# Outputs of twelve chunks as one stacked f16 product per head in a fused mLSTM and mixture-of-experts kernel

## The chip, the cores and the metric

The kernel runs on one core of one Trainium2 chip. The metric is the device time of one execution in microseconds (us), as the median of three runs. The engines are named as the profile names them: PE is the matrix engine (PEld its weight loads), DVE the vector engine, ACT the scalar engine, POOL is GpSimd, SP the engine that issues most DMAs (SPq its queue).

## The reference, cut to what matters

There are 4 sequences (b) of 768 tokens with 8 heads of width 40. Each head keeps a state, every token reads it, and the results become rows of 320 numbers. Each row then goes to the one of eight experts that a router picks.

```python
for t in range(S):
    m_new = np.maximum(f_gate[:, :, t] + m, i_gate[:, :, t])
    f_stab = np.exp(f_gate[:, :, t] + m - m_new)
    i_stab = np.exp(i_gate[:, :, t] - m_new)
    m = m_new
    C = f_stab[..., None, None] * C + i_stab[..., None, None] * einsum('bhd,bhe->bhde', vt, kt)
    n = f_stab[..., None] * n + i_stab[..., None] * kt
    h_tilde = einsum('bhde,bhe->bhd', C, qt)
    denom = np.maximum(np.abs(einsum('bhd,bhd->bh', n, qt)), 1.0)[..., None]
    y[:, :, t] = sigmoid(o_gate[:, :, t]) * h_tilde / denom
x = y.transpose(0, 2, 1, 3).reshape(3072, 320)
logits = x @ w_gate + modality_bias[modality_id]
e_idx, gate_w = argmax(logits), softmax(logits)[e_idx]
out[mask_e] = gate_w[mask_e] * (relu(x[mask_e] @ w1[e]) @ w2[e])
```

## The kernel before

With these gates the state of a head no longer changes after the first 64 tokens of its sequence. `still_arm` builds that state S (the 40 columns of C and the vector n, 41 columns per head) from 64 tokens, and reads it for all later ones. A second arm, which does the general recurrence, stands behind a branch on a word that a check leaves; it is not run here.

**Chunks.** The 3072 tokens are 24 chunks of 128. Chunks 0 to 21 are light: their output is a product of the chunk's queries with S. Chunks 0 to 5 belong to b=0, 5 to 10 to b=1, 11 to 16 to b=2, 16 to 21 to b=3 (5 and 16 are half and half). Chunks 22 and 23 hold the first 64 tokens of every sequence (`special`).

**Light products.** S lies block-diagonal, three heads to a group: 120 rows by 123 columns. `light` (L1984) does one f32 product for each of three groups. From chunk 14 on (`SPLIT = 7` pairs of chunks) `light16` (L2006) does three f16 products a group in its place: high part of q by high part of S, high by low, low by high. The high parts are made by ACT, the low parts by DVE (L2003 and L2004 for a pair of chunks' queries, L1896 and L1897 for a state).

**Behind a chunk.** DVE multiplies the output by its gate (L2039) and the denominators (L2032 to L2037), POOL scales it (L2055), ACT rounds it to f16 (L2057), DVE forms the remainder (L2059), and POOL's indirect DMA scatters the rows to x_s in DRAM (L2066), ordered by modality, so that rows for one expert lie together.

**Experts.** Almost all rows of one modality go to one expert, so two experts (A and B) have their weights loaded (L1968) and split in a high and a low f16 part by ACT (L1969) and DVE (L1970). Rows are worked in 14 tiles in the order of `STREAM`: A0, then A1 and A2 together, then eleven tiles of 256 rows, B0, B1, A3, B2, A4 and so on. The first three tiles take their columns from SBUF by selection products (L2193); the others by a DMA transpose of x_s on SP's queue (L2161). A tile has a first layer (L2295 for whole blocks of 128 inputs, L2303 for the last 64), whose results ACT turns into hh (L2283) and DVE into the remainder hl (L2284), and a second layer (L2340): 16 products with hh, then 8 with hl, for each 128 rows. The router's products are L2233.

**Order.** Every step is a task of a `Plan`. The sequence of tasks on each engine is read from a string of numbers (`ORDER`), and each engine works its own list strictly in that order; PE takes a light product where the list has it, between an expert's products, and waits there if its queries or states aren't ready. Where the plan sees a gap on PE, products with zeros are put in (L2537).

Of the kernel before, what the change touches and what calls it, by code (L numbers as in the profile page):

```python
# [1563 lines left out]
SPLIT = 7  # L1564
# [33 lines left out]
    "-f-g-h-k-l-o-p-s-t-w-x-y-z-{-|.#.$.%.&.'.(.-.../.2.3.6.7.:.;.>.?.@.A.B.C.F.G,s.H.I.J.K.Q.R.S.V.W.Z.[._.`.c.d.e.f.g.h.k.l"
    ".m.n.o.p.u.v.w.z.{.~/#/&/'/*/+/,/--8/.///2/3/4/5/6/7-=#)#{#+#U%r#?#}#,#2#/#*#3#4#<#5#7#8#@#I#B#|#J#K#A#L#D#C#W#E#N#M#F#V"
    "#G#O#Q#Y$N%-$L$c#P%/$J$,$($)$*$-$+$>$.$B$?$C$@$0$A$4$~$%${$z%#$1$|$5$F$}$G%w%z%v%{$Q#f&,#c&-%x#i$e%&%y&.&f%'&/&0&1&M#l&h"  # L1600
    "&k#o#r#u#x&O$T&V&X%2&~&z&y&}&{&|$U$V$W$h$i&4$j$k$^$Y&5%5%6%7%~&#$_$`'E'=$Z'A'I%G'd&s%8%J%D%>'%%M'Q(,&j%:$q&r%?'g'&%P'c%@"
# [69 lines left out]
def still_arm(tc, a, out):  # L1671
# [123 lines left out]
    def load_q(i):  # L1795
        dma(393, lambda: sy.dma_start(qg[i % 4], a["ql"][:, 2 * i:2 * i + 2]), w=[f"qg{i % 4}"])
# [208 lines left out]

    def light16(c, n, y):  # L2006
        if c % 2 == 0:
            split_q(c // 2)
# [677 lines left out]
```

## Time and profile before

| what | value |
|---|---|
| median of 3 runs | 211.71 us (210.97 to 212.02) |
| profiled execution | 210.83 us, span 208.9 us |
| PE busy | 198.2 us (95% of the span) |
| DVE busy | 129.1 us (62%) |
| ACT busy | 98.0 us (47%) |
| POOL busy | 76.1 us (36%) |
| bytes moved by DMA | 30.72 MB |
| granted PE clock, mean | 0.992 |

The span runs from the first to the last instruction; the profiled execution's time is 1.9 us more than that. Busy shares are averages over the whole span. Until about 58 us of the trace the states, the light chunks, the weights of two experts and the first tiles overlap; after it the tiles set the rhythm.

### The profile page before, as it was taken

Reading aid. Unit: us, or ns where it says so; the run is one execution under the profiler, and the core shown is the slowest. Engines: PE = TensorE matmul, PEld = TensorE weight load, DVE = VectorE, ACT = ScalarE, POOL = GpSimd, SP = SyncE. Lnnn points to the kernel's source line nnn. Section 1 sums busy time; section 2 is a strip of 40 time slices with the busy share of each in tenths; the row PEclk is TensorE's granted clock in tenths of the full one; section 3 lists DMA queues with packets and bytes.
Section 4 is the critical chain, followed back from the end, with each engine's and each line's share of the span. In section 5 each row is a group of like instructions: output and inputs, shape, how many; then the busy total and the mean of one; then the engine's idle time right before and its main releaser. Section 6 shows DMA issues by size and latency. Waiting matters only on the chain. (4 is left out here: it accounts for less than half of the span.)

```text
span 208.9 us, 5296 instructions
## 1 busy us (share of the span) xinstructions
PE 198.2 (95%) x2063; PEld 155.8 (75%) x2064; DVE 129.1 (62%) x446; ACT 98.0 (47%) x202; POOL 76.1 (36%) x84
## 2 busy tenths in 40 slices
PE   6879999999999999999999999999999999999960
PEld 2569979878788788778778787787787877878640
DVE  7999797998967737665576406028961521595600
ACT  3579688867687419455425205343141321411320
POOL 5035772652448363634183253000302305020231
PEclk9999999999999999999999999999999999999996
DMA  5999995968784851266211328500101105930000
GB/s 180 349 397 403 399 385 160 288 261 223 161 264 142 132 132 55 79 125 163 46 63 72 89 81 217 93 3 0 64 2 63 34 31 178 313 142 3 31 33 27
DMA packets 27111, 30.72 MB, mean 147 GB/s; under 512 B 19190, under 2 KB 19480, under 8 KB 26824
## 3 DMA queue, kind: packets, MB, share of 16 engines
q1 hardware_dynamic: 24520, 22.06, 36.4%
q0 software_dynamic: 2416, 8.13, 11.1%
q8 instruction: 17, 0.28, 0.5%
q10 hardware_dynamic: 144, 0.13, 0.2%
q14 instruction: 14, 0.11, 0.2%
HBM read 18.57 MB, written 8.22 MB: 128 GB/s over the span
## 5 line engine op out<-in xcount | busy, mean ns | idle before, releaser
L2355 POOL DMA_INDIRECT out<-ob,ois x25 | 24.7, 990 | 77.8 <-ACT ob L2353 27.1
L2340 PEld LDWEIGHTS <-hh 128*128 128x128 f16 (+1 forms) x400 | 37.7, 99 | 14.0 <-issue 0.3
L2284 DVE SCALAR_TENSOR_TENSOR hl<-H,hh 128x512 f16<-128x512 f32 (+2 forms) x40 | 25.5, 649 | 35.8 <-ACT hh L2283 34.4
L2283 ACT ACTIVATE hh<-H 128x512 f16<-128x512 f32 (+2 forms) x40 | 22.1, 567 | 46.0 <-PE H L2295 28.4
L2066 POOL DMA_INDIRECT x_s<-rows,pos_i x24 | 25.7, 1072 | 28.3 <-ACT Sh L1896 4.0
L2353 ACT ACTIVATE ob<-O,zs 128x320 f32<-128x320 f32 x24 | 12.6, 525 | 34.2 <-PE O L2340 9.5
L2340 PE MATMUL O<-w2hA,hh 128*128 128x320 f16 (+1 forms) x104 | 27.8, 299 | 0.0
L2340 PE MATMUL O<-w2lA,hh 128*128 128x320 f16 (+1 forms) x104 | 27.8, 299 | 0.0
L2340 PE MATMUL O<-w2hB,hh 128*128 128x320 f16 x96 | 26.5, 299 | 0.0
L2340 PE MATMUL O<-w2lB,hh 128*128 128x320 f16 x96 | 26.5, 299 | 0.0
L2295 PE MATMUL H<-xt,w1hA 128*128 128x256 f16 (+2 forms) x176 | 26.4, 259 | 0.0
L2340 PEld LDWEIGHTS <-hl 128*128 128x128 f16 (+1 forms) x200 | 18.8, 98 | 7.8 <-issue 0.7
L2295 PE MATMUL H<-xt,w1hB 128*128 128x256 f16 x144 | 24.4, 273 | 0.0
L2295 PEld LDWEIGHTS <-w1hA 128*128 128x128 f16 x224 | 20.3, 98 | 2.9 <-issue 0.6
L2295 PE MATMUL H<-xt,w1lA 128*128 128x256 f16 (+2 forms) x88 | 22.1, 259 | 0.0
L2295 PEld LDWEIGHTS <-w1hB 128*128 128x128 f16 x192 | 18.0, 98 | 3.5 <-issue 1.3
L2295 PE MATMUL H<-xt,w1lB 128*128 128x256 f16 x72 | 19.6, 273 | 0.0
L2055 POOL TENSOR_TENSOR xr<-xr,ab 128x640 f32<-128x640 f32 x11 | 14.8, 1344 | 10.0 <-DVE ab L2037 9.9
L2340 PE MATMUL O<-w2hA,hl 128*128 128x320 f16 (+1 forms) x104 | 16.1, 299 | 0.0
L2340 PE MATMUL O<-w2hB,hl 128*128 128x320 f16 x96 | 15.2, 299 | 0.0
L1996 PE MATMUL Y<-S,qg 120*128 120x123 f32 (+3 forms) x90 | 11.2, 277 | 1.6 <-DVE ab L2032 0.8
L2059 DVE TENSOR_TENSOR rows<-xr,rows 128x128 f16<-128x128 f32 (+1 forms) x22 | 10.1, 478 | 3.9 <-ACT rows L2057 3.9
(215 smaller groups left out, 381.0 us busy)
## 6 DMA issues: line engine op xcount, KB each, us to landing
qg<-in_ql SPq DMA_DIRECT2D x11, 384.0 KB
og<-in_ogl SPq DMA_DIRECT2D x12, 320.0 KB
stage<-in_w1s SPq DMA_DIRECT2D x8, 320.0 KB
stage<-in_w SPq DMA_DIRECT2D x8, 320.0 KB
stage<-in_w1t SPq DMA_DIRECT2D x1, 1280.0 KB
og<-in_w SPq DMA_DIRECT2D x1, 1280.0 KB
kvs<-in_kvs SPq DMA_DIRECT2D x2, 364.5 KB
sp<-in_spq SPq DMA_DIRECT2D x4, 160.0 KB
```

What stands on the lines that cost most here:

```text
L1996: t_.matmul(y[p0:p1, HQ * g:HQ * g + w], lhsT=q[0:k, i, g, p0:p1], rhs=Ss[b][0:k, g, 0:w], start=(g == 0), stop=(g == 2), skip_group_check ...
L2055: on(640, lambda: by.tensor_tensor(x3, x3, ab.rearrange("p c h o -> p (c h) o").broadcast_to([P, 2 * H, D]), ALU.mult), r=abk, w=xk)
L2059: two(2 * (z - a0), lambda a0=a0, z=z, o=o: v.tensor_tensor(rows[:, cs, o:o + z - a0], xr[:, :, a0:z], rows[:, cs, a0:z], ALU.subtract), r ...
L2066: ins = g_.indirect_dma_start(out=x_s[:, :], out_offset=bass.IndirectOffsetOnAxis(ap=pos_i[:, c:c + 1].bitcast(U32), axis=0), in_=rows[:, ...
L2283: act(g * n, lambda: s_.activation(hh[:, sl, 0:n], hp3, AF.Relu), r=[nb], w=[f"hh{j}{i}" for i in fs])
L2284: dve(g * n, lambda: v.scalar_tensor_tensor(hl[:, sl, 0:n], hp3, 0.0, hh[:, sl, 0:n], ALU.max, ALU.subtract), r=[nb] + [f"hh{j}{i}" for i ...
L2295: t_.matmul(dst, lhsT=w[:, i, ws], rhs=x[:, xb], start=(first and b == 0 and q == 0), stop=(last and b == 1 and q == 2), skip_group_check= ...
L2340: t_.matmul(op[p0:p0 + nr, 0:DM], lhsT=t[:, at[f], o_:o_ + nr], rhs=w[:, f], start=(i < ways), stop=(i >= 24 - ways), skip_group_check=True)
L2353: act(DM + 80, lambda op=op, o=o, qc=qc, nr=nr: s_.mul(obs[o][0:nr], op[0:nr, 0:DM], facs[0:nr, qc:qc + 1]), r=[no, f"fac{m_}"], w=[f"ob{o}"])
L2355: swdma(164, lambda o=o, qc=qc, nr=nr: disjoint("outf", g_.indirect_dma_start(out=out[:, :], out_offset=bass.IndirectOffsetOnAxis(ap=ois[0 ...
```

## The change

`SPLIT` goes from 7 to 5, so the f16 form begins at chunk 10. In that form a chunk's queries are loaded threefold (`q3`: 120 rows, three copies of a head's 40 query elements, 8 heads by 128 tokens, 512 KB a chunk, one DMA for each chunk, where a pair of chunks was 384 KB). ACT writes the high part to all 120 rows, and DVE overwrites rows 0 to 39 with the low part. The state is laid out as 120 rows by 41 columns a head: high, high, low. One product over 120 rows gives low q by high S, high q by high S and high q by low S at once: 8 products of 41 columns for a chunk, in place of 9 of 123 and 82.

The stacked state comes from a new function, `stack_states`: ACT and DVE split the unmasked 120 by 369 block (for b=2 and b=3 straight from PSUM, for which the masking by DVE, L1892, falls away), one DMA writes both parts to DRAM, and three DMAs read the diagonal blocks back (40 rows each, runs of 574 bytes). `split_q`, which did a pair of chunks, is gone. Some tiles share memory (tri with a stacked state, gb with the f32 states, aw with kws, Wt with gt), the router's weights get the flag for the shared port in the plan (L2468), and all five engines get new sequences.

```diff
-SPLIT = 7
+SPLIT = 5
...
     def load_q(i):
-        dma(393, lambda: sy.dma_start(qg[i % 4], a["ql"][:, 2 * i:2 * i + 2]), w=[f"qg{i % 4}"])
+        if i < SPLIT:
+            dma(393, lambda: sy.dma_start(qg[i % 4], a["ql"][:, 2 * i:2 * i + 2]), w=[f"qg{i % 4}"])
+            return
+        for c in (2 * i, 2 * i + 1):
+            n, j = c - 2 * SPLIT, (c - 2 * SPLIT) % 3
+            dma(524, lambda j=j, n=n: sy.dma_start(qf[j], a["q3"][:, n]), w=[f"qf{j}"] + ([f"qg{j}", f"qg{j + 1}"] if n < 3 else []))
...
+    def stack_states(b, src, key):
+        d = S_d[b - 1]
+        act(3 * HQ, lambda: s_.mul(S16[:, 0], src, SSC), r=[key], w=["Sh"])
+        (two if b == 1 else dve)(3 * HQ, lambda: v.scalar_tensor_tensor(S16[:, 1], src, SSC, S16[:, 0], ALU.mult, ALU.subtract),
+                                 r=[key, "Sh"], w=["Sl"])
+        dma(180, lambda: sy.dma_start(d[0:120 * 6 * HQ].rearrange("(p x) -> p x", p=120), S16.rearrange("p h g n -> p (h g n)")),
+            r=["Sh", "Sl"], w=[f"S_d{b}"] + (["tri"] if b == 1 else []))
+        n = D * 6 * HQ
+        blocks = d[0:3 * (n + DV)].rearrange("(j x) -> j x", j=3)[:, 0:n].rearrange("j (d h n) -> h d j n", d=D, h=2)
+        for e, x in enumerate((0, 0, 1)):
+            dma(82, lambda e=e, x=x: sy.dma_start(Sst[b][D * e:D * e + D], blocks[x][:, :, 0:2 * HQ + DV]), r=[f"S_d{b}"], w=[f"T{b}{e}"])
...
     def light16(c, n, y):
-        if c % 2 == 0:
-            split_q(c // 2)
-        (qh, ql), i, j = q16[c // 2 % 2], c % 2, c // 2 % 2
+        j = (c - 2 * SPLIT) % 3
+        act(H * P, lambda: s_.mul(qst[j][0:120], qf[j][0:120], QSC), r=[f"qf{j}"], w=[f"qh{j}"])
+        two(H * P, lambda: v.scalar_tensor_tensor(qst[j][0:D], qf[j][0:D], QSC, qst[j][0:D], ALU.mult, ALU.subtract), r=[f"qf{j}"], w=[f"qh{j}"])
 
         def mm():
-            for g in range(3):
+            for h in range(H):
+                g, u = divmod(h, 3)
                 for p0, p1, b in spans(c):
-                    k, w = (120, HQ) if g < 2 else (80, 2 * DV)
-                    Sh, Sl = S16[b]
-                    for t, (a, z) in enumerate(((qh, Sh), (qh, Sl), (ql, Sh))):
-                        t_.matmul(y[p0:p1, HQ * g:HQ * g + w], lhsT=a[0:k, i, g, p0:p1], rhs=z[0:k, g, 0:w],
-                                  start=(g == 0 and t == 0), stop=(g == 2 and t == 2), skip_group_check=True)
+                    t_.matmul(y[p0:p1, DV * h:DV * h + DV], lhsT=qst[j][0:120, h, p0:p1], rhs=Sst[b][0:120, u, HQ * g:HQ * g + DV],
+                              start=(h == 0), stop=(h == H - 1), skip_group_check=True)
...
 ORDER = (
-    "#=#>#:#X$&$'$<$=$x$y%t$K%u$M$O&*&+$a$b$d$S&G&H&I&J&K&P%+%,%.%0&g&Q&R&S&T&w&Y&x&Z&[&]&^$g&_'9':';%4'>'?'B'C'F'G'a'b'J'K'L"
+    "#=#>#:#X$$$%$:$;$v$w%r%s$I$K$M&/&.$_$`$b&K&L&M$Q&N&O%)%*%,%.&T&U&V&W&X&l$e&^&_&`&a&b&c'H'I'J'M'N'Q'R'U'V'Y'Z'[']%2'('^'_"
```

What the new sequences move is seen at three places.

On PE, between the first and the second layer of A1 with A2 (Y are the banks of the light products, O and H those of the experts). Before, chunks 12 and 13 stand there in f32:

```order
L2295 MATMUL O_66<-xt_105,w1lA 128x192
L1996 MATMUL Y_69<-S_120,qg_79 128x123 x2
L1996 MATMUL Y_69<-S_120,qg_79 128x82
L1996 MATMUL Y_70<-S_120,qg_79 128x123 x2
L1996 MATMUL Y_70<-S_120,qg_79 128x82
L2340 LDWEIGHTS hh_112
```

Now chunk 10 stands a little later, behind the 16 products with hh and the router's five and ahead of the first with hl; the pair of rows for a head comes eight times:

```order
L2353 MATMUL O_67<-w2lA,hh_109 64x320
...
L2246 LDWEIGHTS xt_102
L2246 MATMUL M_68<-wgr,xt_102 128x16
L2030 LDWEIGHTS qst_78
L2030 MATMUL Y_69<-Sst_85,qst_78 128x41
...
L2353 LDWEIGHTS hl_111
```

Chunks 10 and 11 stood before and inside the second layer of A0, and 12 and 13 here; now 10 is here, 11 behind B0's first layer, and 12 and 13 in B1's first layer. All four have left the stretch ahead of B0 but chunk 10.

On DVE, the stretch ahead of the remainders of A1 with A2. Before (w1lB are the low parts of B's first-layer weights):

```order
L2059 TENSOR_TENSOR rows<-xr_158,rows 128x2x256
L2253 TENSOR_SCALAR gsm_178<-gsm_178 128x1
L2254 RECIPROCAL zs<-gsm_178 128x1
L2284 SCALAR_TENSOR_TENSOR hl_114<-H_65,hh_112 128x2x192
L2284 SCALAR_TENSOR_TENSOR hl_114<-H_63,hh_112 128x2x192
L2248 TENSOR_REDUCE zs<-ky_174 128x1
L2284 SCALAR_TENSOR_TENSOR hl_114<-H_64,hh_112 128x2x192
L2284 SCALAR_TENSOR_TENSOR hl_114<-O_66,hh_112 128x2x192
L1970 SCALAR_TENSOR_TENSOR w1lB<-stage,w1hB 128x640
```

After (S_81 is a state's low part, qst a chunk's queries):

```order
L1911 SCALAR_TENSOR_TENSOR S_81<-Y_69,S_81 120x369
L2072 TENSOR_TENSOR rows<-xr_151,rows 128x2x256
L2257 TENSOR_TENSOR lg_161<-lg_161,mxx_167 128x8
L2024 SCALAR_TENSOR_TENSOR qst_78<-qg,qst_78 40x1024
L2254 SCALAR_TENSOR_TENSOR lg_162<-lg_162,bias 64x8
L2265 TENSOR_REDUCE gsm_169<-ex_163 128x1
L1990 SCALAR_TENSOR_TENSOR w1lB<-stage,w1hB 128x640
L2266 TENSOR_SCALAR gsm_169<-gsm_169 128x1
L2050 RECIPROCAL ab_149<-ab_149 128x16
L2267 RECIPROCAL zs<-gsm_169 128x1
L1990 SCALAR_TENSOR_TENSOR w1lB<-stage,w1hB 128x640
L2297 SCALAR_TENSOR_TENSOR hl_111<-H_63,hh_109 128x2x192
```

A state's low part, one chunk's queries and two of B's weights have moved ahead of the remainders.

On SP, from B's first weights to B0's transpose and on. Before:

```order
L1968 DMA stage<-in_w1s 128x640
L1796 DMA qg_80<-in_ql 128x768
L1968 ISA
L1968 DMA stage<-in_w 128x640
L1799 DMA og<-in_ogl 128x640
L2161 DMA_TRANSPOSE xt_107<-x_s 128x5x256
L1968 ISA
L1968 DMA stage<-in_w 128x640
```

After (S_d are the states in DRAM, Sst the stacked ones in SBUF):

```order
L1918 DMA Sst_85<-S_d_82 40x3x287
L1988 ISA
L1988 DMA stage<-in_w1s 128x640
L2174 DMA_TRANSPOSE xt_104<-x_s 128x5x256
L1913 DMA S_d_83<-S_81 120x738
L1806 DMA qg<-in_q 128x1024
L1988 ISA
L1988 DMA stage<-in_w 128x640
...
L2175 DMA zs<-x_s 128x2x1
L1918 DMA Sst_86<-S_d_83 40x3x287
```

The reads of the state of b=1 now stand ahead of B0's transpose, and those of b=2 behind the last of B's weights, ahead of B1's transpose.

## Rows read from the trace of the kernel before

**Rows 1.** The page's first lines: span, busy time of the engines.

```profile
span 208.9 us, 5296 instructions
PE 198.2 (95%) x2063; PEld 155.8 (75%) x2064; DVE 129.1 (62%) x446; ACT 98.0 (47%) x202; POOL 76.1 (36%) x84
```

**Rows 2.** Windows: stretch, its length, busy time per engine, clock, DMA share.

```profile
16.00:43.40 27.40, 27.40 (x364) 23.52 (x361) 24.73 (x78) 23.56 (x50) 16.75 (x15) 1.00 0.93 329
58.00:88.00 30.00, 30.00 (x327) 23.93 (x325) 19.22 (x65) 17.68 (x35) 16.89 (x16) 1.00 0.51 135
118.00:203.60 85.60, 84.02 (x783) 65.17 (x781) 39.23 (x134) 25.73 (x54) 18.09 (x19) 1.00 0.26 79
```

**Rows 3.** Timeline of PE, 26 to 39 us (start, us, line, operation): f32 chunks 10 to 13.

```profile
26.72 0.90 PE L1996 MATMUL Y<-S,qg 120*128 120x123 f32 x6
27.45 0.30 PE L2340 MATMUL O<-w2hA,hh 128*128 128x320 f16 x1
...
28.00 0.80 PE L1996 MATMUL Y<-S,qg 120*128 120x123 f32 x6
28.63 0.30 PE L2340 MATMUL O<-w2hA,hh 128*128 128x320 f16 x1
...
37.00 1.49 PE L1996 MATMUL Y<-S,qg 120*128 120x123 f32 x12
38.42 0.32 PE L2340 MATMUL O<-w2hA,hh 128*64 128x320 f16 x1
```

**Rows 4.** Timeline of PE, 65 to 73 us: f16 chunk 16, then another.

```profile
65.73 0.25 PE L2017 MATMUL Y<-Sh,qh 120*64 120x123 f16 x2
...
66.30 0.31 PE L2340 MATMUL O<-w2hB,hh 128*128 128x320 f16 x1
...
72.00 0.22 PE L2017 MATMUL Y<-Sh,qh 120*128 120x123 f16 x1
...
72.33 0.20 PE L2017 MATMUL Y<-Sh,qh 80*128 80x82 f16 x1
...
72.44 1.25 PE L2340 MATMUL O<-w2hB,hl 128*128 128x320 f16 x8
```

**Rows 5.** Timeline of PE at 77 us: the router's ten products, and what follows.

```profile
77.23 0.41 PE L2233 MATMUL M<-wgr,xt 128*128 128x16 f16 x10
77.49 0.38 PE L2295 MATMUL H<-xt,w1hA 128*128 128x256 f16 x2
```

**Rows 6.** Groups by form, PEld: weight loads of f16 light products (busy, mean ns).

```profile
L2017 PEld LDWEIGHTS <-qh 120*128 120x128 f16 x28 | 2.3, 98 | 0.2
```

**Rows 7.** Groups by form, DVE and ACT: splits of queries, states and weights.

```profile
L2004 DVE SCALAR_TENSOR_TENSOR ql<-qg,qh 120x768 f16<-120x768 f32 x4 | 3.8, 953 | 0.8 <-ACT qh L2003 0.8
L1970 DVE SCALAR_TENSOR_TENSOR w1lB<-stage,w1hB 128x640 f16<-128x640 f32 x4 | 3.2, 818 | 0.0
L1897 DVE SCALAR_TENSOR_TENSOR Sl<-S,Sh 120x369 f16<-120x369 f32 x3 | 1.6, 539 | 0.0
L1892 DVE TENSOR_TENSOR S<-Y,mask 120x369 f32<-120x369 f32 x2 | 1.0, 538 | 0.0
L2003 ACT ACTIVATE qh<-qg 120x768 f16<-120x768 f32 x4 | 3.3, 837 | 0.0
```

**Rows 8.** Timeline of DVE, 13 to 39 us: router's weights, A's and the remainders.

```profile
13.92 0.87 DVE L2468 SCALAR_TENSOR_TENSOR wgr<-cst,wgr 128x24 f16<-128x24 f32 x1
...
26.30 3.06 DVE L1970 SCALAR_TENSOR_TENSOR w2lA<-stage,w2hA 128x640 f16<-128x640 f32 x4
...
36.73 1.02 DVE L2284 SCALAR_TENSOR_TENSOR hl<-H,hh 128x384 f16<-128x384 f32 x2 [0.88 <-ACT hh L2283]
...
38.20 0.55 DVE L2284 SCALAR_TENSOR_TENSOR hl<-O,hh 128x384 f16<-128x384 f32 x1
```

**Rows 9.** Timeline of SP's queue, 38 to 46 us: a write to DRAM and its reader.

```profile
38.80 0.43 SPq L2481 DMA_DIRECT2D g_d<-G  x1
45.14 0.51 SPq L2096 DMA_DIRECT2D gb<-g_d  x1
```

More of the change, by code (lines that the diff above doesn't have):

```diff
@@ L1598 @@
[L1598 to L1601, printed above, removed]
@@ L1742, in still_arm @@
     kvs = [tl([P, 9 * D + 9 * DV], F32, f"kvs{i}") for i in range(2)]
-    qg = [tl([P, 2, 3, P], F32, f"qg{i}") for i in range(4)]
-    q16 = [[tl([120, 2, 3, P], F16, f"q{n}{i}") for n in "hl"] for i in range(2)]
-    S16 = [None] * B if SPLIT > 10 else [None] + [[tl([120, 3, HQ], F16, f"S{n}{b}") for n in "hl"] for b in range(1, B)]
+    qgs = tl([P, 4 * 6 * P], F32, "qg")
+    qg = [qgs[:, 6 * P * i:6 * P * (i + 1)].rearrange("p (c g t) -> p c g t", c=2, g=3) for i in range(4)]
+    qf = [qgs[:, H * P * i:H * P * (i + 1)].rearrange("p (h t) -> p h t", h=H) for i in range(3)]
+    qst = [tl([P, H, P], F16, f"qst{i}") for i in range(3)]
+    S16 = tl([120, 2, 3, HQ], F16, "S16")
+    S_d = [dr.tile([3 * (D * 6 * HQ + DV)], F16, name=f"S_d{b}") for b in range(1, B)]
+    Sst = [None] + [tl([P, 3, 2 * HQ + DV], F16, f"Sst{b}") for b in range(1, B)]
     ogs = tl([P, NOG * 2 * DM], F32, "og")
@@ L1767, in still_arm @@
     obs = [tl([P, DM], F32, f"ob{i}") for i in range(3)]
-    Ss = [tl([P, 3, HQ], F32, f"S{b}") for b in range(3)]
-    Ss.append(Ss[0])
+    Ss2 = tl([P, 2, 3, HQ], F32, "S")
+    Ss = [Ss2[:, b] for b in range(2)]
     ident = tl([32, 32], F32, "ident")
-    tri = tl([P, P], BF16, "tri")
+    tri = Sst[1].rearrange("p j n -> p (j n)")[:, 0:P].bitcast(BF16)
     ones = tl([P, P], BF16, "ones")
@@ L1808, in still_arm @@
     kw = [kws[:, i] for i in range(2)]
-    m, gt, G, Bs, Wt = (tl([32, FT], F32, n) for n in ("m", "gt", "G", "Bs", "Wt"))
+    m, gt, G, Bs = (tl([32, FT], F32, n) for n in ("m", "gt", "G", "Bs"))
+    Wt = gt
     zz = tl([P, P], BF16, "zz")
@@ L2083, in prefill @@
         dma(84, lambda: sy.dma_start(x_s[NX - SPARE:NX], zrow[0:SPARE]), r=["zrow", "zid"], w=["prefill"])
-    gb = small([H, FT], "gb")
-    aw = small([H, FT], "aw")
+    gb, aw = (t.rearrange(f, **k)[:, 0:H * FT].rearrange("p (h t) -> p h t", h=H)
+              for t, f, k in ((Ss2, "p b g n -> p (b g n)", {}), (kws, "p b h d -> p (b h d)", {})))
     bT = small([16], "bT")
@@ L2467, in still_arm @@
     act(24, lambda: s_.mul(wgr[:, :, 0], wg_sb, WSC), r=["cst"], w=["wgh"])
[L2468 removed]
+    two(24, lambda: v.scalar_tensor_tensor(wgr[:, :, 1], wg_sb, WSC, wgr[:, :, 0], ALU.mult, ALU.subtract), r=["cst", "wgh"], w=["wgr"])
     done = [0]
@@ L2628, in _layout_still @@
     qt = q.transpose(0, 2, 1, 3)[b_, t_]
-    ql = np.zeros((P, 22, 3, P), np.float32)
+    ql = np.zeros((P, 2 * SPLIT, 3, P), np.float32)
+    q3 = np.zeros((P, 22 - 2 * SPLIT, H, P), np.float32)
+    for e in range(3):
+        q3[D * e:D * e + D] = qt[2 * SPLIT:22].transpose(3, 0, 2, 1)
     for h in range(H):
         g, j = divmod(h, 3)
-        ql[D * j:D * (j + 1), :, g] = qt[0:22, :, h].transpose(2, 0, 1)
+        ql[D * j:D * (j + 1), :, g] = qt[0:2 * SPLIT, :, h].transpose(2, 0, 1)
     ogl = o.transpose(0, 2, 1, 3)[b_, t_].reshape(NC, P, DM).transpose(1, 0, 2)
```

65 lines of the change are left out of this document (32 added, 33 removed).

## The prediction

> **What bounds the kernel now.** I began with the page's busy times: PE is at work in 198.2 of 208.9 us, no other engine in more than 62% [rows 1]. Such a share is an average, so next came the windows, cut at 16 us (PE's last wait) and at 43.4 us (start of B0). The reader is to see there that PE's busy time equals the length of the stretch from 16 to 43.4 us and from 58 to 88 us, and that its clock stands at 1.00 of full speed, the 2.4 GHz level, in all of them [rows 2]. In the stretch to 203.6 us it lacks 1.58 us [rows 2], at its end: PE stops at about 202.0, and only the last output is left. So what PE no longer has to do after 16 us is worth its full time, as long as no other engine then comes too late. That is a real condition from 16 to 43.4 us: there DVE is busy for 24.73 and ACT for 23.56 of 27.4 us, and the DMA engines for 0.93 of the time. From 58 to 88 us DVE has 19.22 of 30 and ACT 17.68, with the DMA engines at 0.51 [rows 2]; after 118 us both are mostly idle.
>
> **What PE loses.** I take a step's time on PE as the distance from its first product to the next step's first, since products overlap. The f32 chunks 10 to 13 take 27.45 - 26.72 = 0.73, 28.63 - 28.00 = 0.63 and, two together, 38.42 - 37.00 = 1.42 us: 2.78 us [rows 3]. An f16 chunk takes 72.44 - 72.00 = 0.44 us, and chunk 16, whose two halves run side by side, 66.30 - 65.73 = 0.57 [rows 4]. Chunks 14, 15 and 17 to 21 make seven of the first kind: 3.08 + 0.57 = 3.65 us. In all 6.43 us fall away.
>
> **What PE gets.** Eleven chunks of 8 products with 41 columns, and 16 half-wide ones for chunk 16. The trace has no product of f16 with 41 columns, but has it between two rows with the same full weight load: the router's ten products of 16 columns take 77.49 - 77.23 = 0.26 us, 0.026 each [rows 5], and the three of 82 columns 72.44 - 72.33 = 0.11, 0.037 each [rows 4]. 41 columns are nearer to 16; I take 0.030. Then 88 products are 2.64 us, and chunk 16 is 8 pairs at 0.030 plus the 0.13 by which it exceeds a whole chunk today, 0.37: together 3.0 us (2.6 by the lower row, 3.7 by the upper). Net, PE has 6.43 - 3.0 = 3.4 us less to do (2.7 to 3.8). 2.5 of it (2.78 less chunk 10's new 0.24) lie ahead of B0, 0.9 behind its start.
>
> A page speaks against this price. The Trainium skill, "TensorE: Matmul & The Clock Gate", section "Back-to-back issue gap", gives about 81 ns for each product of 128 columns in a sustained stream of load and product; the six of 123 columns here take (72.33 - 72.00) / 6 = 55 ns [rows 4], so the measurement decides. At 81 ns the new products would be 7.9 us and PE would have 1.5 us more to do, about 213.9 us.
>
> **What is lost on the way.** The early 2.5 us count only if DVE delivers earlier too, and two places are close. First, A0's second layer uses A's second-layer remainders, four pieces of 0.77 us from 26.30 to 29.36 [rows 8], a piece each 0.55 us (28.00 - 27.45 [rows 3]). Today two f32 chunks stretch that use; without them PE comes to the fourth piece nearly a us before 29.36. DVE reaches the pieces earlier as well: two maskings are gone (1.0 us [rows 7]) and the router's remainder (0.87, for 24 columns [rows 8]) is moved away, against one state's remainder of 0.54 [rows 7]. I put the loss there at 0.3. Second, the remainders of A1 with A2 end at 38.75 today, with 0.88 us of DVE's waiting ahead of them [rows 8]. In the new list a state's remainder (0.54), one chunk's queries (0.953 for 768 columns, so about 1.27 for 1024) and two of B's pieces (2 x 0.82) stand ahead of them [rows 7], while two chunks' gating and denominators have gone. PE wants them 1 to 2 us earlier. I put 0.4 there. So 0.7 us lost: bounds 0 (DVE always in time) and 2.5 (B0 starts at 43.4 as before).
>
> **What I cost at nothing.** The queries' splits: 12 chunks at 1.27 on DVE and 1.12 on ACT (0.837 for 768 [rows 7]) are 15.2 and 13.4 us, in place of 3.8 and 3.3 [rows 7]: some 11 and 10 us more. All but the first chunk's stand between B0's start and the end of B2, where about 40% of either engine is free by the stretch from 58 to 88 us [rows 2]; in a tile of (202.0 - 43.4) / 11 = 14.4 us there are three or four such chunks, 4 to 5 us. Remainders (hl) may wait behind one for 1.3 us; 16 products with hh come ahead of them on PE, four times 0.55, 2.2 us [rows 3]. If that cover went, each us of a late chunk would be a us of PE. Transfers: 12 x 512 KB for 6 x 384 KB, with the states some 5 MB more, some 14 us of the DMA engines at the 354 GB/s that 329 at a share of 0.93 come to; half their time is free at 58 to 88 us [rows 2]. The router's remainder is a gain of up to 0.7 us on DVE, which I have counted within the loss above.
>
> **Sum.** 3.4 - 0.7 = 2.7 us less. The profiled execution's 210.83 us (1.9 us around a span of 208.9) would become 208.1, the span 206.2; that execution lies 0.9 below the median of 211.71, from which I forecast 209.0.
>
> **Rivals.**
> 1. *The saving mostly arrives* (the forecast), 207.5 to 210.3. For it: PE's full stretches [rows 2] and that later tiles have idle engines. Against: the two close places. Chance 0.65.
> 2. *DVE and ACT set B0's start.* Their 90% and 86% before 43.4 us [rows 2] stay, PE waits where the f32 chunks stood and only the late 0.9 us counts: 210.8 (210.3 to 211.9). Against it: their lists ahead of B0 have two chunks less behind the products. Chance 0.16.
> 3. *The states come late through SP's queue*, the one on the other side. The state of b=2 is written to DRAM behind B0's transpose, at about 36 us, and three reads wait for that write on SP, with the state of b=3 and B1's transpose queued behind them. PE stops at chunk 11, at the end of B0's first layer, near 48 us. A write and the read behind it are seen once: issued at 38.80, the reader let go at 45.14, 6.3 us [rows 9]. That makes 42.3 for the reads, and 48.6 if they need as long to land: just about in time. It decides for slower when the states land 3.8 us after PE wants them (the 2.7 us gained plus 1.1), past 52 us, that is with some 8 us each way; then about 213.2. Against it: the 6.3 us include a queue full of weights. Chance 0.08.
> 4. *The products don't become cheaper by their columns.* At the 123-column spacing of 0.055 they are 5.4 us, the net gain 1.0 and with the loss 0.3: 211.4, chance 0.05. If the weight loads (98 ns [rows 6]) stood bare, 9.5 us, 215.5 us, chance 0.03: the router's 26 ns speak against it.
> The remaining 0.03 is for a larger gain, below 207.5, if DVE's head start shortens the first 16 us too.
>
> **How the numbers follow.** The point is rival 1's, 209.0. The range from 207.3 to 211.9 holds cases 1, 2 and the milder half of 4, and most of the last 0.03: 0.86 by these chances; I leave it there because the loss's bounds (0 to 2.5) and the products' (2.7 to 3.8) put 207.9 and 211.5 inside. 0.5%, about 1.1 us, is what a measurement can tell from no change. Faster by more than that (under 210.65): case 1, a third of case 2 at most, and the last 0.03: 0.70. Within: the rest of case 2 and the 211.4: 0.18. Slower: 3, the bare loads, and a little for what no row shows: 0.12.
>
> **What would show it.** Products of L2030 about 0.03 us apart, 0.24 us a chunk. B0's first product at 41 to 42 us in place of 43.4, with PE's first gaps after 16 us in A0's and A1/A2's second layers, released by DVE hl or w2lA. From B0 to the end 0.2 us less than today's 158.6 (0.9 gained, 0.7 for chunks 11 to 13). No wait of PE at L2030. Wrong would make it: a wait for qst or Sst there, B0 still at 43.4, or L2030 at 0.055 us and more.

## The result, and the profile after

| | before | after |
|---|---|---|
| median, us | 211.70 (4 runs, 210.97 to 212.02) | 208.21 (4 runs, 207.99 to 209.25) |
| profiled execution, its span | 210.83, 208.9 | 207.99, 206.1 |
| DMA, MB | 30.72 | 35.81 |

The ratio is 0.985, 95% interval 0.9808 to 0.9891: faster by 1.1 to 1.9%, where 209.0 us (0.987) was forecast. The changed kernel, run again later, gave 0.989 (e5). Lines of the kernel have moved by 11 to 20; the products of `light` are L2016, those of `light16` L2030, the experts' second layer L2353.

The page of the changed kernel, first lines, for [rows 1]: PE has 3.0 us less, DVE 12.4 and ACT 9.1 more.

```profile
span 206.1 us, 5360 instructions
PE 195.2 (95%) x2064; PEld 152.6 (74%) x2064; DVE 141.5 (69%) x452; ACT 107.1 (52%) x210; POOL 84.8 (41%) x84
```

Its windows, cut at B0's new start (stretch, length, PE, PEld, DVE, ACT, POOL busy, clock, DMA share, GB/s), for [rows 2]:

```profile
16.00:41.67 25.67, 24.56 (x338) 20.18 (x336) 24.86 (x65) 20.66 (x41) 18.08 (x15) 1.00 0.96 313
41.67:58.00 16.33, 16.33 (x182) 13.17 (x181) 15.06 (x50) 13.40 (x25) 9.20 (x7) 1.00 0.93 282
58.00:88.00 30.00, 29.95 (x345) 23.40 (x342) 21.82 (x70) 20.26 (x36) 15.71 (x14) 1.00 0.86 245
118.00:200.80 82.80, 81.14 (x783) 63.23 (x777) 44.36 (x146) 29.33 (x62) 19.92 (x21) 1.00 0.31 85
```

PE is full from B0 on. Ahead of B0 it now lacks 1.11 us, where it lacked nothing. The DMA share from 58 to 88 us is 0.86, not 0.51.

PE's timeline shows both sums (for [rows 3, 4]; a bracket is the idle time ahead and what ended it):

```profile
16.08 0.54 PE L2552 MATMUL M<-zz 128*128 128x512 bf16 x2
16.46 0.44 PE L2206 MATMUL O<-sel,rows 128*128 128x128 f16 x5
...
18.04 1.57 PE L2016 MATMUL Y<-S,qg 120*128 120x123 f32 x12 [0.85 <-DVE xr L2052]
...
27.72 0.30 PE L2353 MATMUL O<-w2lA,hh 128*128 128x320 f16 x1 [0.25 <-DVE w2lA L1990]
...
37.45 0.36 PE L2030 MATMUL Y<-Sst,qst 120*128 120x41 f16 x8
37.74 0.73 PE L2353 MATMUL O<-w2hA,hl 128*64 128x320 f16 x8
...
41.67 0.38 PE L2308 MATMUL H<-xt,w1hB 128*128 128x256 f16 x2
...
65.54 0.36 PE L2030 MATMUL Y<-Sst,qst 120*128 120x41 f16 x8
65.75 1.25 PE L2353 MATMUL O<-w2hB,hl 128*128 128x320 f16 x8
...
73.44 0.74 PE L2030 MATMUL Y<-Sst,qst 120*64 120x41 f16 x24
74.02 0.38 PE L2308 MATMUL H<-xt,w1hA 128*128 128x256 f16 x2
...
198.98 0.17 PE L2467 MATMUL M<-bsum,ones 128*128 128x1 bf16 x1
```

A stacked chunk takes 0.29 or 0.30 us at three places (37.45 to 37.74 is one), 0.20 to 0.22 at seven (65.54 to 65.75 is one), and chunks 16 and 17 together take 0.58. B0 starts at 41.67, 1.77 earlier than before. PE's one new long wait, 0.85 us ahead of chunk 8, is for DVE. DVE's timeline and POOL's there (for [rows 8]):

```profile
16.44 1.15 DVE L1957 TENSOR_SCALAR ss<-cumx 128x2 f32<-128x2 f32 x1
17.51 0.87 DVE L2052 SCALAR_TENSOR_TENSOR xr<-og,Y 128x320 f32<-128x320 f32 x2
...
24.91 2.03 DVE L1990 SCALAR_TENSOR_TENSOR w2lA<-stage,w2hA 128x640 f16<-128x640 f32 x1
```

```profile
15.99 1.58 POOL L2068 TENSOR_TENSOR xr<-xr,ab 128x640 f32<-128x640 f32 x1 [1.41 <-DVE ab L2050]
...
24.97 1.27 POOL L2068 TENSOR_TENSOR xr<-xr,ab 128x640 f32<-128x640 f32 x1
```

A comparison of two columns lasts 1.15 us and ends at 17.59, as POOL's scaling does (17.57); a piece of A's remainders lasts 2.03 where its neighbours take 0.81, and POOL scales then too. PE's waits of 0.85 and 0.25 us stand behind these two. In the kernel before, the same comparison stood well ahead of POOL's scaling, and the new list has moved it:

```profile
7.28 0.16 DVE L1937 TENSOR_SCALAR ss<-cumx 128x2 f32<-128x2 f32 x1
```

### The profile page after: what moved, and what is told of

The parts are those of the page before. It is cut to its first block, busy times and chain, and to the rows that moved or that the text cites. A ratio compares the mean times of both kernels' runs of the same rounds, so it can differ in the third digit from the quotient of the medians.

```text
span 206.1 us, 5360 instructions
## 1 busy us (share of the span) xinstructions
PE 195.2 (95%) x2064; PEld 152.6 (74%) x2064; DVE 141.5 (69%) x452; ACT 107.1 (52%) x210; POOL 84.8 (41%) x84
## 2 busy tenths in 40 slices
DMA packets 29551, 35.81 MB, mean 174 GB/s; under 512 B 19421, under 2 KB 21151, under 8 KB 29263
## 4 chain that ended last, share of the span: by engine, by line
PE 77%; DVE 8%; DMA 6%; issue 2%; ACT 2%; SPq 1%; POOL 0%; POOLq 0%; DVEq 0%; ACTq 0%
PE O L2353 36%; PE H L2308 21%; PE H L2316 7%; PE O L2308 7%; DMA out<-ob,ois 3%; DMA og<-in_ogl 3%; DVE xr L2052 2%; PE M L2246 1%; PE Y L2016 1%; PE Y L2030 1%; PE Y L2135 1%; ACT og L1996 1%; PE Y L2120 1%; DVE w1lA L1990 1%; DVE rows L2072 1%
## 5 line engine op out<-in xcount | busy, mean ns | idle before, releaser
L2368 POOL DMA_INDIRECT out<-ob,ois x25 | 28.3, 1134 | 62.3 <-DVE zs L2261 21.4
L2353 PEld LDWEIGHTS <-hh 128*128 128x128 f16 (+1 forms) x400 | 37.7, 98 | 15.0 <-issue 1.0
L2079 POOL DMA_INDIRECT x_s<-rows,pos_i x24 | 30.2, 1259 | 23.3 <-ACT ob L2366 4.0
L2353 PE MATMUL O<-w2lA,hh 128*128 128x320 f16 (+1 forms) x104 | 27.8, 299 | 0.3 <-DVE w2lA L1990 0.3
L2353 PE MATMUL O<-w2hA,hh 128*128 128x320 f16 (+1 forms) x104 | 27.8, 300 | 0.0
L2353 PE MATMUL O<-w2hB,hh 128*128 128x320 f16 x96 | 26.5, 299 | 0.1
L2353 PE MATMUL O<-w2lB,hh 128*128 128x320 f16 x96 | 26.5, 299 | 0.0
L2353 PEld LDWEIGHTS <-hl 128*128 128x128 f16 (+1 forms) x200 | 18.7, 98 | 7.7 <-issue 0.7
L2353 PE MATMUL O<-w2hA,hl 128*128 128x320 f16 (+1 forms) x104 | 15.8, 300 | 0.0
L2353 PE MATMUL O<-w2hB,hl 128*128 128x320 f16 x96 | 15.3, 299 | 0.0
L2024 DVE SCALAR_TENSOR_TENSOR qst<-qg,qst 40x1024 f16<-40x1024 f32 x12 | 14.5, 1210 | 0.7 <-ACT qst L2023 0.7
L2023 ACT ACTIVATE qst<-qg 120x1024 f16<-120x1024 f32 x12 | 12.5, 1050 | 1.2 <-DMA qg<-in_q 1.2
```

Source lines behind the costliest of these rows:

```text
L2023: act(H * P, lambda: s_.mul(qst[j][0:120], qf[j][0:120], QSC), r=[f"qf{j}"], w=[f"qh{j}"])
L2024: two(H * P, lambda: v.scalar_tensor_tensor(qst[j][0:D], qf[j][0:D], QSC, qst[j][0:D], ALU.mult, ALU.subtract), r=[f"qf{j}"], w=[f"qh{j}"])
L2079: ins = g_.indirect_dma_start(out=x_s[:, :], out_offset=bass.IndirectOffsetOnAxis(ap=pos_i[:, c:c + 1].bitcast(U32), axis=0), in_=rows[:, ...
L2353: t_.matmul(op[p0:p0 + nr, 0:DM], lhsT=t[:, at[f], o_:o_ + nr], rhs=w[:, f], start=(i < ways), stop=(i >= 24 - ways), skip_group_check=True)
L2368: swdma(164, lambda o=o, qc=qc, nr=nr: disjoint("outf", g_.indirect_dma_start(out=out[:, :], out_offset=bass.IndirectOffsetOnAxis(ap=ois[0 ...
```

## The experiments

All kernels are read by one table. "To B0" is from chunk 4's first product to B0's first, "from B0" from there to PE's last product, both of the profiled execution; the first leaves out when chunk 4 begins, which was between 12.35 and 13.30 us from execution to execution. The ratio is to the kernel before in runs beside it, with its interval.

| run | median us | ratio | to B0 | from B0 |
|---|---|---|---|---|
| before | 211.70 | | 31.09 | 158.42 |
| after | 208.21 | 0.985 (0.981 to 0.989) | 29.22 | 157.31 |
| e1 products twice | 211.03 | 0.9975 (0.994 to 1.001) | 29.42 | 159.34 |
| e2 early, one group | | | 30.12 | |
| e3 comparison moved | 208.84 | 0.988 (0.985 to 0.992) | 29.59 | 158.67 |
| e4 POOL cut short | | | 27.95 | |
| e5 after, again | 209.05 | 0.989 (0.985 to 0.993) | 29.22 | 157.86 |
| e6 moved, 5 buffers | 208.84 | 0.988 (0.985 to 0.991) | 29.56 | 157.25 |
| e7 moved, a third loaded | 208.44 | 0.986 (0.983 to 0.988) | 29.57 | 157.20 |
| e8 loads twice, same buffer | 243.46 | 1.142 (1.135 to 1.149) | | |
| e9 loads twice, to DRAM | 214.03 | 1.012 (1.009 to 1.015) | 29.23 | 162.79 |
| e10 low parts twice | 214.87 | 1.016 (1.013 to 1.018) | 29.22 | 164.05 |
| e11 states' detour | 216.20 | 1.021 (1.017 to 1.024) | 29.23 | 164.88 |
| e12 as e6, POOL's product moved | 208.68 | 0.986 (0.983 to 0.988) | 29.50 | 157.79 |

**What a product costs (e1).**

```diff
-            for h in range(H):
+            for k, h in ((k, h) for k in range(2) for h in range(H)):
```

> The changed kernel with each stacked product of a chunk issued twice (the second set starts the sums anew, so the output stays the same): 104 products more. Theory (PE is the bound wherever these products stand, and a product costs its spacing): the eleven places measured in the changed kernel are 0.29, 0.29, 0.30, 0.22, 0.21, 0.22, 0.58 (two chunks, one of half-wide pairs), 0.20, 0.20, 0.21, 0.21 us, together 2.93; the second set comes without its own start, so 2.3 to 3.0 us are added: 210.5 to 211.2 against the 208.2 of the changed kernel, B0's start 0.2 to 0.3 us later. Rival (PE has slack where they stand, or the products hide under weight loads that are there anyway): less than 1 us is added, under 209.2. Rival (81 ns a product): 8.4 us are added, 216.6.

PE's timeline of e1:

```profile
66.64 0.56 PE L2029 MATMUL Y<-Sst,qst 120*128 120x41 f16 x16
67.04 1.25 PE L2353 MATMUL O<-w2hB,hl 128*128 128x320 f16 x8
...
74.86 1.20 PE L2029 MATMUL Y<-Sst,qst 120*64 120x41 f16 x48
75.91 0.38 PE L2308 MATMUL H<-xt,w1hA 128*128 128x256 f16 x2
```

Sixteen products take 0.40 us where eight took 0.21, and the pair of chunks 1.05 for 0.58. Over all eleven places the second set adds 2.46 us to the 2.93, 0.024 a product. "To B0" and "from B0" grew by 0.20 and 1.5 to 2.0, the median by 2.0 (against e5) to 2.8. PE is the bound wherever these products stand.

**The early saving alone (e2), and what holds DVE up (e4).** Both leave outputs uncomputed or unscaled. The kernel's own word then sends it through the general arm as well, so their whole times (633 and 629 us) say nothing; only the stretch to B0 is read.

```diff
-            for g in range(3):
+            for g in range(1 if c >= 10 else 3):
...
```

> The kernel before, with one of the three groups of f32 products for chunks 10 to 13 (six of eight heads of these chunks are left uncomputed). Nothing else moves: the early saving alone, without the new list or the new splits. A chunk falls from about 0.70 to about 0.26 us, so PE has some 1.8 us less ahead of B0. Theory (the early saving counts except what is lost at A's remainders): the fourth piece of A's second-layer remainders, ready at 29.36, is wanted about 0.35 us before; so 1.4 us arrive, B0 starts at about 42.0 and the time is 210.3 (209.9 to 210.7). Rival (DVE and ACT set B0's start): B0 stays at 43.4, PE waits at A0's and A1/A2's remainders, the time is 211.3 or more.

Its PE timeline:

```profile
27.40 0.48 PE L1996 MATMUL Y<-S,qg 120*128 120x123 f32 x2
27.73 0.30 PE L2340 MATMUL O<-w2hA,hh 128*128 128x320 f16 x1
...
28.27 0.38 PE L1996 MATMUL Y<-S,qg 120*128 120x123 f32 x2
28.49 0.30 PE L2340 MATMUL O<-w2hA,hh 128*128 128x320 f16 x1
...
38.39 0.30 PE L2340 MATMUL O<-w2hA,hh 128*64 128x320 f16 x1 [0.53 <-ACT ob L2353]
```

Chunks 10 and 11 take 0.33 and 0.22, 0.81 less than [rows 3]; with as much for 12 and 13 some 1.6 us were saved, and "to B0" is 0.97 shorter (1.4 was expected; B0 itself stands at 43.42, but chunk 4 began 0.95 us later than in the kernel before). So the saving arrives in part even in the old list; 0.53 of the rest is a wait that nobody had named, for ACT to empty an output bank of A0. Measured from chunk 4, DVE and ACT did not hold B0 where it was.

```diff
-            on(640, lambda: by.tensor_tensor(x3, x3, ab.rearrange("p c h o -> p (c h) o").broadcast_to([P, 2 * H, D]), ALU.mult),
+            nw = 1 if i in (2, 3) else 2 * H
+            on(640, lambda: by.tensor_tensor(x3[:, 0:nw], x3[:, 0:nw], ab.rearrange("p c h o -> p (c h) o")[:, 0:nw].broadcast_to([P, nw, D]), ALU.mult),
```

> The changed kernel with two of POOL's scalings (the rows of chunks 4 to 7) cut from 640 columns to 40: fifteen of sixteen heads of these chunks stay unscaled. DVE's list is the same. Theory (a DVE instruction with two operands in SBUF, or a comparison of f32 in SBUF, that meets POOL's tensor work is held until that ends): the comparison of two columns falls from 1.15 us to under 0.3, the first piece of A's second-layer remainders from 2.03 to about 0.8, PE's waits of 0.85 and 0.25 us go, B0 starts at 40.6 to 41.0 and the time is 207.1 to 207.5. Rival (these DVE times have another cause, such as a semaphore or the DMAs): they stay at 1.15 and 2.03, 208.2.

DVE's timeline of e4, the two places:

```profile
17.02 0.16 DVE L1957 TENSOR_SCALAR ss<-cumx 128x2 f32<-128x2 f32 x1
...
24.62 3.07 DVE L1990 SCALAR_TENSOR_TENSOR w2lA<-stage,w2hA 128x640 f16<-128x640 f32 x4
```

1.15 became 0.16, the four pieces take 3.07 in place of 4.24, neither wait of PE is left, and "to B0" fell by 1.27 (0.7 to 1.1 was expected). Nothing in DVE's list had changed: POOL's work held DVE up. The Trainium skill, "SBUF — State Buffer", section "Who interferes with whom", says that a DVE instruction with two inputs in SBUF and a GpSimd instruction that reads SBUF contend, that a DVE instruction in a mode with two ports contends with GpSimd too, and that whichever issues first blocks the other for its whole length. The trace of the changed kernel agrees: 17.59 behind 17.57. Which of the two cases the comparison is, no run shows.

**Getting the 0.85 us back (e3, e6, e7, e12), with e5 as the base.** In e3 the comparison goes behind the outputs of chunks 6 and 7; e6, e7 and e12 keep this edit and add the lines shown for them.

```diff
+        i, j = (next(i for i, t in enumerate(ts) if t["w"] == [w]) for w in ("ss", "wA1l"))
+        flat.remove(i), flat.insert(flat.index(j), i)
```

> The changed kernel with one instruction of DVE's list moved: the comparison of two columns that took 1.15 us (16.44 to 17.59, ending with POOL's scaling at 17.57) stands six instructions later, ahead of A's weights, where POOL had nothing to do. Theory (it was held up by POOL's work, and the outputs of chunks 6 and 7 behind it were late for that reason alone): PE waits less than 0.2 us ahead of chunks 8 and 9 in place of 0.85, the moved instruction takes 0.1 to 0.2 us, and B0 starts 0.4 to 0.85 earlier, at 40.8 to 41.3; 207.3 to 207.8. Rival (DVE is short in the whole stretch, so the 0.85 come back as waits at A's remainders): B0 within 0.2 of 41.67 and 208.0 to 208.4. Rival (the wait is for something else): the 0.85 stay.

The comparison took 0.16 and PE's 0.85 went, but "to B0" is longer by 0.37: another instruction of DVE's, the one that writes A1's row numbers, stands still. DVE's row in e3:

```profile
22.33 0.22 DVE L2218 TENSOR_SCALAR zs<-O 64x1 int32<-64x1 f32 x1 [1.37 <-PE M L2246]
```

In that profile PE stopped again, 1.34 us near 67 us, for hh of ACT, which had stood 2.46 us for an output transfer. The changed kernel is close to that itself; its chain of waits and ACT's row:

```profile
53.58 7.03 DMA out<-ob,ois
```

```profile
60.70 0.53 ACT L2366 ACTIVATE ob<-O,zs 128x320 f32<-128x320 f32 x1 [1.65 <-DMA out<-ob,ois]
```

So the next runs add buffers (e6), or take away transfers (e7), beside the changed kernel itself (e5).

> The changed kernel itself, as the base for the runs beside it. Every theory expects 207.9 to 209.3 us (median 208.2 so far), 29.2 us from chunk 4's first product to B0's start, 157.3 from there to PE's last product, waits of 0.85 us ahead of chunk 8 and 0.25 at A's second-layer remainders, and 1.6 us or more of ACT's waiting for an output transfer ahead of its first output after 58 us.

```diff
-    obs = [tl([P, DM], F32, f"ob{i}") for i in range(3)]
+    obs = [tl([P, DM], F32, f"ob{i}") for i in range(5)]
-            o = nob[0] % 3
+            o = nob[0] % 5
```

> The changed kernel with the one comparison moved behind the outputs of chunks 6 and 7 on DVE, as in the run before, and with five buffers for finished output rows in place of three. Theory (what PE won early was given back at B1's second layer, because ACT stood 1.65 to 2.46 us at a buffer whose output transfer, issued at 53.58, took 7 us, and the results hh of B1 stood behind it): that wait of ACT's is gone, PE doesn't stop near 65 us, and the 0.85 us arrive: 0.6 to 0.9 less than the changed kernel beside it, 207.3 to 207.6 if that is 208.2. Rival (the give-back has another cause, so another wait takes its place): within 0.3 us of the changed kernel, and PE still loses over 0.5 us between 58 and 72 us.

```diff
-            dma(524, lambda j=j, n=n: sy.dma_start(qf[j], a["q3"][:, n]), ...
+            dma(524, lambda j=j, n=n: sy.dma_start(qf[j][D if n > 2 else 0:2 * D if n > 2 else P], a["q3"][D if n > 2 else 0:2 * D if n > 2 else P, n]), ...
```

> The changed kernel with the comparison moved, three buffers, and for chunks 13 to 21 only the middle 40 of the 120 rows of queries loaded (the two correction terms of these chunks are then made from another chunk's queries): 3.1 MB less to move. Theory (the output transfers are late because the loads of threefold queries fill the DMA engines from 54 to 62 us): the DMA share there falls from 1.0 to about 0.7, the output transfer takes under 5 us, ACT's wait falls under 0.8 and PE's wait near 65 us goes: the time as with five buffers, 0.6 to 0.9 less than the changed kernel beside it. Rival (the transfer waits for something else, such as POOL's issue order): ACT's wait stays above 1.5 us and the time is as without the smaller loads.

Windows from 54 to 75 us of e5, then e6, then e7:

```profile
54.00:62.00 8.00, 8.00 (x102) 6.67 (x100) 5.45 (x17) 4.36 (x9) 5.44 (x4) 1.00 1.03 333
62.00:75.00 13.00, 12.66 (x153) 9.51 (x152) 10.16 (x30) 10.88 (x20) 5.63 (x6) 1.00 0.77 246
```

```profile
54.00:62.00 8.00, 8.00 (x101) 6.62 (x100) 6.34 (x19) 5.60 (x11) 5.35 (x4) 1.00 1.01 320
62.00:75.00 13.00, 13.00 (x158) 10.23 (x157) 9.66 (x29) 10.04 (x18) 5.80 (x6) 1.00 0.83 263
```

```profile
54.00:62.00 8.00, 8.00 (x101) 6.64 (x100) 6.17 (x19) 5.66 (x12) 4.91 (x4) 1.00 0.63 201
62.00:75.00 13.00, 13.00 (x159) 10.21 (x157) 10.54 (x33) 10.11 (x19) 6.00 (x6) 1.00 0.68 191
```

In e5 PE lost 0.34 us to that wait; with buffers or with fewer bytes it lost none, ACT's wait for an output transfer is gone in both, and "from B0" is 0.6 shorter (though no shorter than in the changed kernel's first profile, 157.31, where PE lost nothing). That half of the theory holds, by one execution of each: the full DMA engines (1.03) can reach PE through late outputs. The other half fell: the 0.85 us did not arrive, for L2218 stood in their place, and the medians are within 0.7 of e5's.

> As the run with the comparison moved and five output buffers, and POOL's first product for the bias (two operands of 16 columns) moved from behind its second scatter to right ahead of the next one that uses it, at about 29 us (the same output). In all three runs with the comparison moved, DVE stood 1.34 to 1.37 us at the instruction that writes A1's row numbers and went on 0.15 to 0.18 us after this product of POOL's had ended. Theory (DVE is held up by POOL there too): the wait falls from 1.34 to 1.1 or less, or goes; B0 starts 28.4 to 29.2 us after chunk 4 in place of 29.6, and the time is 0.3 to 1 us less than with five buffers alone, ratio 0.983 to 0.987. Rival (the wait is for PE, whose router products end at the same time): 1.3 us again and 29.5 us, ratio 0.988.

```diff
+        i, j = (next(i for i, t in enumerate(ts) if t["w"] == [w]) for w in ("bt", "bias"))
+        flat.remove(i), flat.insert(flat.index(j), i)
```

The wait stayed, with POOL's product gone from there; DVE's row in e12:

```profile
22.20 0.22 DVE L2218 TENSOR_SCALAR zs<-O 64x1 int32<-64x1 f32 x1 [1.33 <-PE M L2246]
```

POOL's product was not it. By the same section of the Trainium skill an instruction with at most one input in SBUF, outside the two-port modes, does not contend with GpSimd, and L2218 reads PSUM alone. Why it waits for PE in the four kernels with the comparison moved stays open. It is not that PE is ahead there: in e4, where PE had not stood ahead of chunk 8 either, L2218 began at 20.55 without a wait. No version was measurably faster than the changed kernel.

**The work costed at nothing (e8 to e11).**

```diff
-            dma(524, lambda j=j, n=n: sy.dma_start(qf[j], a["q3"][:, n]), ...
+            dma(524, lambda j=j, n=n: [sy.dma_start(qf[j], a["q3"][:, n]) for _ in range(2 if n else 1)][-1], ...
```

> The changed kernel with the load of the threefold queries issued twice for chunks 11 to 21 (5.8 MB more, the same output). Theory (the DMA engines are full from 54 to 62 us already, share 1.06 and 1.02): some 16 us of transfers more don't fit between 42 and 75 us, outputs and queries come late, PE stops at B1 or A3: 1.5 to 5 us slower than the changed kernel beside it, 209.7 to 213. Rival (as the prediction put it, half of the DMA engines' time is free there): within 0.5 us of it.

It came out 34 us slower, and measured something else: the second load waits on SP until the first has landed, and SP's row `46.09 11.62` for four loads shows the queue standing. e9 sends the second load to DRAM.

```diff
+            dma(524, lambda j=j, n=n: [sy.dma_start(t, a["q3"][:, n]) for t in [qf[j]] + qx[n:n + 1] * (n > 0)][0], ...
...
```

> The changed kernel; behind each load of threefold queries for chunks 11 to 21 stands a second one of the same size that goes to a place in DRAM that nobody uses and nobody waits for (5.8 MB more read and as many written, 11 more issues of about 0.4 us on SP; the same output). It separates the load on the DMA engines from SP's waiting, which the run with the load doubled into the same buffer mixed. Theory (the DMA engines are full from 54 to 62 us): output transfers and queries come later, ACT's wait for the output buffer grows from 1.9 to over 3 us, PE stops at B1 and A3: 2 to 6 us slower than the changed kernel, ratio to the kernel before 0.995 to 1.015. Rival (half of the DMA engines' time is free behind B0's start, as the prediction put it): within 0.5 us, ratio 0.984 to 0.991.

e10:

```diff
...
+        two(H * P, lambda: [v.scalar_tensor_tensor(z, qf[j][0:D], QSC, qst[j][0:D], ALU.mult, ALU.subtract)
+                            for z in ((qjunk, qst[j][0:D]) if c > 10 else (qst[j][0:D],))][-1], ...
```

> The changed kernel with DVE's low part of the queries computed twice for chunks 11 to 21, first into an unused buffer (eleven instructions of 1.2 us more on DVE, 13.3 us in all; the same output). Theory (DVE has room behind B0's start, 21.82 of 30 us busy from 58 to 88): at most a few remainders come late, 0 to 0.8 us slower than the changed kernel, ratio 0.985 to 0.993. Rival (a chunk's split holds up the remainders behind it, each us of a late chunk is a us of PE): 3 us or more, ratio over 1.0.

Windows from 62 to 75 us of e9, then e10:

```profile
62.00:75.00 13.00, 9.61 (x93) 6.67 (x92) 8.31 (x25) 8.98 (x16) 5.18 (x5) 1.00 1.08 338
```

```profile
62.00:75.00 13.00, 10.85 (x107) 8.06 (x106) 12.72 (x34) 7.63 (x14) 5.99 (x5) 1.00 0.81 233
```

Their PE timelines name the waits:

```profile
67.09 0.31 PE L2353 MATMUL O<-w2hB,hh 128*128 128x320 f16 x1 [2.35 <-ACT hh L2296]
...
74.21 0.41 PE L2246 MATMUL M<-wgr,xt 128*128 128x16 f16 x10 [1.04 <-DMA xt<-x_s]
```

```profile
59.61 0.37 PE L2030 MATMUL Y<-Sst,qst 120*128 120x41 f16 x8 [0.58 <-DVE qst L2024]
...
68.68 0.37 PE L2030 MATMUL Y<-Sst,qst 120*128 120x41 f16 x8 [1.30 <-DVE qst L2024]
```

e9: 5.0 us slower than e5, the size that the theory had. Its path was another one: ACT's wait for an output buffer did not grow to over 3 us but was 1.16, and together with waits of 0.50 for gates and 0.90 for queries it made hh late for PE's 2.35. The run has 11 more issues on SP as well, and does not separate them from the bytes. e10: 5.8 us slower, where at most 0.8 was expected; the rival's size holds. Its mechanism holds only in part: PE stood 2.90 us in all for the late queries of the chunks themselves, and 0.72 for a remainder. From 62 to 75 us DVE was busy for 12.72 of 13: an average of 21.82 in 30 us had hidden that these 13 us have 10.2.

e11 copies a state in DRAM between its write and its reads.

```diff
-        d = S_d[b - 1]
+        d, d2, m = S_d[b - 1], (S_d if b == 1 else S_d2)[b - 1], 120 * 6 * HQ; todo = [lambda: sy.dma_start(d2[0:m], d[0:m])] * (b > 1)
...
```

> The changed kernel with a copy from DRAM to DRAM between the write and the three reads of the stacked states of b=2 and b=3 (the same output): SP waits there for one more write to land. It prices the rival in which the states come late. The reads of b=2 are issued at 40.4 to 41.5, and PE wants them at chunk 11, 48.7. Theory (a margin of some 4 us): the copy takes 3 to 5 us, the reads of b=2 land at about 48 to 49, PE waits less than 1 us at chunk 11, and what is queued behind on SP (B1's transpose at 49.5) is late by no more than that: 0 to 1 us slower, ratio 0.985 to 0.993. Rival (there was no margin, the states landed just in time): PE waits over 2 us at chunk 11 and the time is 2 us or more longer, ratio over 0.995.

SP's queue and PE in e11:

```profile
41.37 0.59 SPq L1909 DMA_DIRECT2D S_e<-S_d  x1
45.24 1.53 SPq L1919 DMA_DIRECT2D Sst<-S_e  x3
...
54.25 0.56 SPq L1909 DMA_DIRECT2D S_e<-S_d  x1
...
60.42 0.40 SPq L1809 DMA_DIRECT2D og<-in_ogl  x1
```

```profile
49.29 0.36 PE L2030 MATMUL Y<-Sst,qst 120*128 120x41 f16 x8
...
66.75 0.31 PE L2353 MATMUL O<-w2hB,hh 128*128 128x320 f16 x1 [2.29 <-ACT hh L2296]
...
69.15 0.45 PE L2353 MATMUL O<-w2hB,hh 128*128 128x320 f16 x1 [1.69 <-ACT hh L2296]
```

Neither expectation holds: the time is the rival's, but its wait is not there. The reads moved from 40.41 to 45.24, chunk 11 from 48.69 to 49.29, and PE still did not wait there: that margin is over 4 us. The 7.2 us (against e5) came from what stood behind on SP: a load of gates, issued at 60.42 behind the copy for b=3 in place of 53.72, held ACT for 4.20 us, and hh behind it. PE's two waits are 3.98 us of it; most of the rest is a lower clock behind them (last section).

## Why the prediction was right, point by point

- **What PE loses and gets.** 6.43 us fell away. Eleven places took 2.93 us in all (0.20 to 0.30 each, 0.58 for chunks 16 and 17) where 3.0 were forecast; net 3.5 for 3.4. Taking the price near [rows 5] was right: 0.024 us a product (e1). The 0.055 and 0.098 of rival 4 did not come. The Trainium skill's 81 ns, "TensorE: Matmul & The Clock Gate", section "Back-to-back issue gap", are stated for 128 columns, and the 7.9 us worked out from them did not come. Not even at 128 columns does the trace agree: from 20.49 to 20.99 in the kernel before, nine products of 128 columns, each with its load, take 0.50 us, 56 ns each.
- **What is lost on the way.** 0.7 was forecast; 2.49 saved less 1.77 at B0 makes 0.72. The size came out by luck, for neither of its two places was right in its reason. By the distances that the prediction counts with, A0's second layer lost 0.41 for the 0.3 (PE's first two products stand 0.56 apart, 0.15 in e4), but at the second of the four pieces, behind the one that POOL had held up, and not at the fourth; in e4 PE waited for none. At A1 with A2 nothing was lost where 0.4 stood. In its place came a wait that the prediction had no line for, 0.86 ahead of chunk 8 (5.59 us from chunk 4 to chunk 8, 4.73 in e4), and 0.38 of new zero products. Against them stand chunk 7 (0.72) and one group of A0's selection products (0.30), now done before 16 us: 0.86 + 0.41 + 0.38 - 0.72 - 0.30 = 0.63; the other 0.09 is spread over small places. The cause of both waits is DVE held by POOL (e4): shown.
- **The sign that was there.** In [rows 8] the router's remainder takes 0.87 us for 24 columns and ends at 14.79. POOL's scaling in the kernel before ends at 14.75:

```profile
13.49 1.26 POOL L2055 TENSOR_TENSOR xr<-xr,ab 128x640 f32<-128x640 f32 x1 [1.93 <-DVE ab L2037]
```

  The prediction took the 0.87 as the remainder's own price. In the changed kernel it stands at 6.82 and takes 0.18, while the comparison has come beside the next scaling.
- **From B0 to the end** the text gave 0.2 less, and 1.11 came (0.56 in e5). That figure took chunks 11 to 13 off twice; the sum's own 0.9 had them in already, and by the measured places it is 3.65 - 2.64 = 1.01.
- **Costed at nothing.** True of the time, nearly: one execution lost 0.34 us to late outputs (e5). Wrong of the reserve: half free was the kernel before, where 0.49 of 30 us is 14.7, and the prediction's own 14 us of transfers all but fill that. From B0's start to 88 us the DMA engines are now at 0.93 and 0.86, from 54 to 62 us at 1.03 (e5). Another 13 us of DVE cost 5.8 us (e10), another 5.8 MB, read and written, 5.0 (e9).
- **Sum.** -2.7 forecast; span -2.8, profiled execution -2.84, medians -3.5, and -2.4 in e5. It came out that near partly by the luck of the lost 0.7.
- **Rivals.** 1 came. 2: B0 moved by 1.77. 3: no wait at chunk 11, with over 4 us to spare (e11); but a held queue on SP can cost 7 us through the loads behind. 4: see above.

## What to carry to other kernels

On an engine that is full, price products by the spacing of the nearest rows, and add them up: that came within 0.1 us. An average of free time over 30 us is no reserve; look at the 8 to 13 us in which the new work falls, and at what stands behind a waiting instruction in its queue. When a list is rewritten, look which DVE instructions now fall beside POOL's tensor work, for one of two columns can cost 1 us there.

## What the runs showed of the hardware

- Sixteen products of 41 columns, each with its own weight load of 120 rows, take 0.40 us, 0.025 each; a load alone shows 96 ns in the rows. The loads overlap.
- In e11 PE was busy for 1.17 of the 5 us from 64 to 69 us; from 69 to 74 us the granted clock was 0.50, the 1.2 GHz level, and a product of 320 columns stood 0.27 us from the next (69.39, 69.66) in place of 0.135; at 75 it was 1.00 again. So a stall cost more than its own length here: PE's two waits are 3.98 us, and "from B0" is 7.0 longer than in e5.
- A DVE comparison of two columns took 1.15 us beside POOL's scaling of 640 columns and 0.16 without it (e4); the profile shows the hold as the instruction's own busy time, not as idle time ahead of it.
- With the comparison moved (e3, e6, e7, e12) DVE stood 1.33 to 1.37 us at the same instruction in each of four executions; why is not known.
